# The k/q stage, the sum of z and the attention loop of a transformer block's backward pass, rearranged

## The chip, the cores and the metric

The kernel runs on one core of one Trainium2 chip. The metric is the time of one execution on the device in microseconds (us), the median of several runs. A core has five engines with their own instruction queues: TensorE (matmuls; PE in the profile, PEld its weight loads), VectorE (DVE), ScalarE (ACT), GpSimd (POOL) and SyncE (SP, which here issues transfers only). Sixteen DMA engines move data between DRAM and SBUF, the on-chip memory; matmul results go to PSUM.

## The reference, cut to what matters

The reference computes a pre-norm block and all its gradients: linear attention, then a SwiGLU feed-forward part (FFN), each on a layernorm without weights, with residuals. S = 2048 rows, D = 640, 32 heads of 20, F = 1728, all bf16.

```python
def _A_ref(x, wqkv, wo):
    ...                                        # q, k, v of 32 heads
    phi = lambda t: jnp.where(t > 0, t + 1, jnp.exp(t)) + 1e-6
    pq, pk = phi(q), phi(k)
    kv  = jnp.einsum("bhsd,bhse->bhde", pk, v)
    z   = jnp.einsum("bhsd->bhd", pk)          # sum of pk over the 2048 rows
    num = jnp.einsum("bhqd,bhde->bhqe", pq, kv)
    den = jnp.einsum("bhqd,bhd->bhq", pq, z)[..., None] + 1e-6
    return (num / den) ... @ wo

h   = x + _A_ref(_layernorm(x), wqkv, wo)
out = h + (silu(_layernorm(h) @ w_gate) * (_layernorm(h) @ w_up)) @ w_down
# results: out, and by jax.vjp with grad_out the gradients of x, wqkv, wo, w_gate, w_up, w_down
```

## The kernel before, where the change touches it

The rows are 16 tiles of 128. The kernel never forms v or the attention output: with xn the normalised x, Y = xn^T pk (`ps_y`), the masked blocks of Wv^T Y give kv (`ps_kvt`), those times wo give one matrix W2 (`ps_w2t`), and attention is then the normalised q times W2 (`ps_a`). A "dm step" (`ps_dm`) is a matmul of the backward pass, grad_out times w_down transposed, that depends on nothing here and is strewn in: 24 steps of 10 matmuls in all. PSUM has four tiles named `mm`, given out in turn, so a matmul group can start only when the group four places earlier has been read out.

The k/q stage, tile by tile. Tiles up to 10 have their normalised x transposed by TensorE (`copy1`), the last five by a DMA transpose that SyncE issues. The dictionary `after` sets at which tile SyncE issues the stores and the later loads.

```python
XD = 11
BY_V = (1, 2, 3, 6, 9)
...
def kq_mm(t, which, between=None, pieces=((0, DT),)):
    ...                                  # 10 matmuls ps_kq of 320 columns
    nc.scalar.activation(out=half(dst[:, t, :]), in_=row(ps), func=ACT.Exp, scale=sc)
    nc.scalar.activation(out=half(rr[...]), in_=row(ps), func=ACT.Relu, scale=sc)

def phi(which, t, n=2):
    e = (pk, pqa)[which][:, t:t + n, :]
    nc.vector.tensor_scalar(out=e, in0=e, scalar1=1.0, scalar2=1e-6, op0=ALU.min, op1=ALU.add)
    nc.vector.tensor_tensor(out=e, in0=e, in1=rr[...], op=ALU.add)
...
def copy1(t):                            # ln1_tr1: 5 transposes ps_t by TensorE
    (nc.vector.tensor_copy if t in BY_V else nc.scalar.copy)(out=xnT[:, t], in_=ln1_tr1(t))
...
for t in range(2, ST):
    ...
    if XD <= t + 2 < ST:
        ln1_xn(t + 2)
        nc.sync.dma_start_transpose(out=xnT[:, t + 2], in_=xn[:, t + 2, :])
    if t > 3 and t + 3 < ST:
        ln1_stats(t + 3)
    kq_mm(t, 0, (lambda: copy1(t + 1)) if t + 1 < XD else None)
    ...
    kq_mm(t, 1)
    ...                                  # phi of the tiles before; last: phi(0, 15), phi(1, 12), phi(1, 14)
    if t + 2 < XD:
        ln1_xn(t + 2)
    ...
    for f, *a in after.get(t, ()):
        f(*a)
```

Y and z. z is summed by TensorE, in four groups of 32 columns side by side; a second small matmul spreads it to all partitions (`zb`). `normalise` divides four tiles of q by their denominators, all on VectorE; `tr_pqs` transposes them by DMA.

```python
def normalise(t):
    ...                                  # tz = pq * zb (bf16), 4 tiles = 2560 elements
    nc.vector.tensor_reduce(out=den[:], in_=hb4(tz), axis=AX.X, op=ALU.add)
    nc.vector.tensor_scalar(out=den[:], ..., scalar1=1e-6, op0=ALU.add)
    nc.vector.reciprocal(out=rall[:, t:t + 4, :], in_=den[:])
    nc.vector.tensor_tensor(out=hb4(pq), in0=hb4(pq), in1=bc4(rall[:, t:t + 4, :]), op=ALU.mult)
...
def z_sum():
    ...                                  # 32 matmuls, lhsT=ones[:, :H], rhs=pk[:, t, n0:n1]
    nc.scalar.copy(out=half(zs[0][:]), in_=row(ps))
    nc.vector.tensor_tensor(out=half(zs[1][:]), in0=row(ps), in1=half(zs[0][:]), op=ALU.subtract)
    nc.vector.memset(KVT, 0.0)

for i in range(DT):                      # 5 column tiles of Y
    ...                                  # 32 matmuls ps_y; z_sum() after the first 16 of i = 0
    if i == 0:
        ...                              # ps_zb: 4 matmuls with ones32 (1/32), then zb
        masks()
    if 0 < i < 4:
        dm(1)
dm(1)
for t in (0, 4):
    normalise(t); tr_pqs(t)
for t in range(6):
    load_xr(t)
...                                      # kv_blocks: 4 x ps_kvt, each masked by VectorE into KVT
dm(1)
for i in range(DT):
    if i % 2 == 0 and i > 0:
        dm(1)
    ...                                  # ps_w2t, read out by ScalarE, transposed by DMA into W2
for t in (8, 12):
    normalise(t); tr_pqs(t)
dm(2)
```

The attention loop, which also makes the second layernorm (`hn`) and its transpose (`hnT`), the FFN's input:

```python
hnT = big.tile(...)
for t in range(ST + 2):
    if t < ST:
        ...                              # 10 matmuls ps_a; at t = 0 dm(1) between its halves
        nc.vector.tensor_tensor(out=half(xr[:]), in0=row(ps), in1=half(xr[:]), op=ALU.add)
        ln_stats(xr[:], mv[:, 0, :]); ln_rstd(mv, rstd2, t, 1)
        if t > 0:
            dm(1)
    if t > 2:
        load_xr(t + 3)
    u = t - 2
    ...
    nc.scalar.dma_start(out=scr_h1_v[:, u, :], in_=h1[:])
    nc.vector.tensor_scalar(out=hn[:, u, :], ...)
    nc.sync.dma_start_transpose(out=hnT[:, :, u * P:(u + 1) * P], in_=hn[:, u, :])
...
wgu = {0: load_wgu(0)}                   # the FFN's first weights
```

Of the kernel before, what the change touches and what calls it, by code (L numbers as in the profile page):

```python
# [20 lines left out]
def kernel(  # L21
# [160 lines left out]
    def load_wgu(g):  # L182
        w = GW[g]
        t = wpool.tile([P, DT, 2 * GM], BF16, name="wgu", tag="wgu")
        nc.sync.dma_start(out=t[:, :, 0:w], in_=B_w_gate[:, GO[g]:GO[g] + w].rearrange("(k p) n -> p k n", p=P))
        nc.sync.dma_start(out=t[:, :, w:2 * w], in_=B_w_up[:, GO[g]:GO[g] + w].rearrange("(k p) n -> p k n", p=P))
        return t
# [30 lines left out]
    def load_3():  # L218
        for t0 in range(4, ST, 2):
            yield load_x(nc.sync, t0, t0 + 2)  # L220
        yield load_wdT(wdT, 0)
        yield load_dh2T(0)
        yield load_dh2T(1)

    def load_dh2T(c):
        return nc.sync.dma_start_transpose(out=dh2T[:, :, c * 512:(c + 1) * 512], in_=go_flat[c * 512:(c + 1) * 512, :])

    def load_wv():
        nc.sync.dma_start(out=wvo[:, 0:5], in_=A_wqkv[:, 2 * D:3 * D].rearrange("(k p) n -> p k n", p=P))

    def load_wo(j0, j1):
        for j in range(j0, j1):
            nc.sync.dma_start(out=wvo[:, 5 + j, :], in_=A_wo[OH[j]:OH[j] + P, :])
# [9 lines left out]
    ones32 = const.tile([P, P], BF16, name="ones32")  # L243
    nc.vector.memset(ones32[:], 1.0 / H)
# [23 lines left out]
    XD = 11  # L268
    BY_V = (1, 2, 3, 6, 9)
# [46 lines left out]
    def phi(which, t, n=2):  # L316
        e = (pk, pqa)[which][:, t:t + n, :]
        nc.vector.tensor_scalar(out=e, in0=e, scalar1=1.0, scalar2=1e-6, op0=ALU.min, op1=ALU.add)
        nc.vector.tensor_tensor(out=e, in0=e, in1=rr[:, 2 * which + t // 2 % 2, t % 2:t % 2 + n, :], op=ALU.add)

    def store_k(c):
        nc.sync.dma_start(out=scr_pk_v[:, 4 * c:4 * c + 4, :], in_=pk[:, 4 * c:4 * c + 4, :])

    def store_q(c):
        nc.sync.dma_start(out=scr_pq_v[:, 4 * c:4 * c + 4, :], in_=pqa[:, 4 * c:4 * c + 4, :])

    def store_x(c):
        nc.sync.dma_start(out=scr_xnT[4 * c:4 * c + 4].rearrange("t p k c -> p t k c"), in_=xnT[:, 4 * c:4 * c + 4])

    after = {5: [(store_q, 0), (store_x, 0)], 6: [(load_dh2T, 2)], 7: [(load_dh2T, 3)], 8: [(load_wv,)], 9: [(store_q, 1)],  # L330
             10: [(store_x, 1)], 11: [(load_wo, 0, 2)], 12: [(load_wo, 2, 4)], 13: [(load_wo, 4, 6), (store_q, 2), (store_x, 2)],
             14: [(store_x, 3), (store_k, 0), (store_k, 1)],
             15: [(store_k, 2), (load_wdT, wdT, 1), (store_q, 3), (store_k, 3), (load_wdT, wdT3, 3)]}

    PIECES = ((0, 3), (3, DT))

    with tc.manual_schedule(engines={EngineType.PE, EngineType.DVE, EngineType.Activation, EngineType.Pool, EngineType.SP}):

        ps = mm("ps_warm")

        def warm(n):
            for _ in range(n):
                nc.tensor.matmul(ps[:, 0, :P], lhsT=ident[:], rhs=ident[:], start=True, stop=True)

        def copies(t, eng_copy):
            for sl, src in ln1_tr(t):
                c = eng_copy(out=xnT[:, t, sl], in_=src)
                if t == 0 and sl.start == 0:
                    wait_for(c, load_3())

        def copy1(t):
            (nc.vector.tensor_copy if t in BY_V else nc.scalar.copy)(out=xnT[:, t], in_=ln1_tr1(t))

        warm(37)
        ln1_stats(0)
        ln1_centre(0, 0, 3 * P)
        ln1_centre(0, 3 * P, D)
        copies(0, nc.scalar.copy)
        warm(8)
        ln1_stats(1)  # L360
        ln1_centre(1)
        kq_mm(0, 0, lambda: copies(1, nc.vector.tensor_copy), PIECES)
        ln1_stats(2)
        ln1_centre(2)
        kq_mm(1, 0, None, PIECES)
        ln1_stats(3)
        kq_mm(0, 1, lambda: copy1(2), PIECES)
        phi(0, 0)
        ln1_xn(3)
        kq_mm(1, 1)  # L370
        for t in range(2, ST):
            if t == 2:
                ln1_stats(4)
            if XD <= t + 2 < ST:
                ln1_xn(t + 2)
                nc.sync.dma_start_transpose(out=xnT[:, t + 2], in_=xn[:, t + 2, :])
            if t > 3 and t + 3 < ST:
                ln1_stats(t + 3)
            kq_mm(t, 0, (lambda: copy1(t + 1)) if t + 1 < XD else None)
            if t == 2:  # L380
                ln1_stats(5)
            if t == 3:
                ln1_stats(6)
            if t == ST - 1:
                phi(0, t - 1, 1)
            kq_mm(t, 1)
            if t == 3:
                phi(1, 0)
            elif t == ST - 1:
                phi(0, t, 1)  # L390
                phi(1, t - 3)
                phi(1, t - 1)
            elif t > 3:
                phi(t % 2, t - 2 - t % 2)
            if t + 2 < XD:
                ln1_xn(t + 2)
            if ST - NC - 1 <= t < ST - 1:
                ln1_xn(t - ST + NC + 1)
            for f, *a in after.get(t, ()):
                f(*a)  # L400

    fA.close()
    fpool = wB.enter_context(tc.tile_pool(name="fpool", bufs=6))
# [33 lines left out]
    def masks():  # L439
        tc.keep_in_program_order(nc.gpsimd.memset(mask[:], 1.0))  # L440
        for c0, n, p0 in ((0, 6, 0), (120, 2, 88)):
            m = mask[:, c0:c0 + n * Dh]
            for sign in (1, -1):
                tc.keep_in_program_order(nc.gpsimd.affine_select(
                    out=m, in_=m, pattern=[[-sign * Dh, n], [0, Dh]], compare_op=ALU.is_ge, fill=0.0,
                    base=-p0 if sign > 0 else p0 + Dh - 1, channel_multiplier=sign))
# [10 lines left out]
    def normalise(t):  # L457
# [7 lines left out]
        nc.vector.reciprocal(out=rall[:, t:t + 4, :], in_=den[:])  # L465
        nc.vector.tensor_tensor(out=hb4(pq), in0=hb4(pq), in1=bc4(rall[:, t:t + 4, :]), op=ALU.mult)

    def tr_pqs(t):
        for tt in range(t, t + 4):
# [9 lines left out]
    with tc.manual_schedule(engines={EngineType.PE, EngineType.DVE, EngineType.SP}):  # L479
        yk = strips.tile([P, DT * D + HG * P], BF16, name="yk", tag="S")  # L480
        Yt = yk[:, :DT * D].rearrange("p (k n) -> p k n", k=DT)
        KVT = yk[:, DT * D:].rearrange("p (j c) -> p j c", j=HG)
        zs = [wk("zs"), wk("zl")]

        def z_sum():
            ps = mm("ps_z")
            for ci, (n0, n1) in enumerate(NCH):
                for t in range(ST):
                    q = t % 4 * H
                    nc.tensor.matmul(ps[q:q + H, ci, :320], lhsT=ones[:, :H], rhs=pk[:, t, n0:n1],  # L490
                                     start=(t < 4), stop=(t >= ST - 4))
            nc.scalar.copy(out=half(zs[0][:]), in_=row(ps))
            nc.vector.tensor_tensor(out=half(zs[1][:]), in0=row(ps), in1=half(zs[0][:]), op=ALU.subtract)
            nc.vector.memset(KVT, 0.0)

        for i in range(DT):
            ps = mm("ps_y")
            for ci, (n0, n1) in enumerate(NCH):
# [3 lines left out]
                if (i, ci) == (0, 0):  # L502
                    z_sum()
            nc.scalar.copy(out=half(Yt[:, i, :]), in_=row(ps))
            if i == 0:
                ps_z = mm("ps_zb")
                mm_row(ps_z, lambda k: ones32[:], lambda k, n0, n1: zs[k][:, n0:n1], 2)
                nc.scalar.copy(out=half(zb[:]), in_=row(ps_z))
                masks()
# [3 lines left out]
        for t in (0, 4):  # L513
            normalise(t)
            tr_pqs(t)
# [14 lines left out]

        kv_blocks(KVT, "ps_kvt", lambda i, a, b: wv[:, i, a:b], lambda i, a, b: Yt[:, i, a:b])

# [3 lines left out]
        for i in range(DT):  # L536
# [5 lines left out]
            nc.sync.dma_start_transpose(out=W2[:, :, i * P:(i + 1) * P], in_=W2T[:, i, :])  # L542
        for t in (8, 12):
            normalise(t)
            tr_pqs(t)
        dm(2)

        hn = big.tile([P, ST, D], BF16, name="hn", tag="B")
        hnT = big.tile([P, DT, S], BF16, name="hnT", tag="B")
        h1s = {}  # L550
        for t in range(ST + 2):
            if t < ST:
# [11 lines left out]
                ln_rstd(mv, rstd2, t, 1)  # L564
                h1s[t] = (xr, mv)
                if t > 0:
                    dm(1)
            if t > 2:
                load_xr(t + 3)
            u = t - 2  # L570
# [9 lines left out]
            nc.scalar.dma_start(out=scr_h1_v[:, u, :], in_=h1[:])  # L580
            nc.vector.tensor_scalar(out=hn[:, u, :], in0=h1[:], scalar1=mv[:, 0, 0:1],
                                    scalar2=rstd2[:, u:u + 1], op0=ALU.subtract, op1=ALU.mult)
            nc.sync.dma_start_transpose(out=hnT[:, :, u * P:(u + 1) * P], in_=hn[:, u, :])


    with tc.manual_schedule(engines={EngineType.SP}):
# [7 lines left out]
        wgu = {0: load_wgu(0)}  # L594
# [7 lines left out]
        for g in range(4):  # L602
# [4 lines left out]
            for t in range(0, ST, 2):  # L607
# [25 lines left out]
                if g == 0 and t == 2:  # L633
                    wait_for(sig, load_dh2())
                    wgu[1] = load_wgu(1)
# [20 lines left out]
            elif g == 1:  # L656
                wgT[0] = big.tile([P, 14, D], BF16, name="wgT", tag="B")
                for gg in range(2):
                    tr_wgT(gg)
                    wgu[gg + 2] = load_wgu(gg + 2)  # L660
# [404 lines left out]
```

## Time and profile before

| | |
|---|---|
| time, median of 3 runs | 820.14 us (818.99 to 820.23) |
| span of the profiled execution | 818.3 us |
| mean granted clock of TensorE | 0.997 of full |
| instructions | 13931 |

The stages in the trace, by the first matmul of each (us from the start of the span):

| stage | from | to |
|---|---|---|
| loads and first k/q tiles | 0 | 11 |
| k/q stage, tiles 2 to 10 | 11 | 39.7 |
| k/q stage, tiles 11 to 15 | 42.0 | 57.4 |
| Y, z, four dm steps | 57.4 | 88.6 |
| kv blocks, W2, five dm steps | 88.6 | 101.0 |
| attention loop, 15 dm steps | 101.0 | 148.9 |
| FFN and all of the backward pass | 148.9 | 818.3 |

How to read what follows: a line of the chain of waits has a start, a length and an instruction group. A line of the list of waits says who waited for whom, then total us, times and the longest. In the table by stretches each engine has its busy us and, in brackets, its instructions. L308 is line 308 of the kernel. The end of a matmul is modelled, and matmuls overlap, so the time from start to start is what one costs TensorE's queue.

### The profile page before, as it was taken

The numbers are of one execution on the slowest core, as the hardware profiler recorded it, in microseconds if no ns is written. First come the engines' busy times: TensorE is split into PE (matmuls) and PEld (weight loads), VectorE is DVE, ScalarE is ACT, GpSimd is POOL, SyncE is SP. The second block draws the span as 40 slices with busy tenths as digits, with TensorE's granted clock in tenths as the row PEclk, the third lists the DMA queues.
The fourth block names the chain that finished last, engine by engine and source line by source line (L and its number), as shares of the span: only waits on it lengthen the run. The fifth ranks groups of instructions, "written<-read, shape, count | busy, mean of one in ns | idle before, by whom it ended". The sixth has DMA issues, their size and how long they took to land.

```text
span 818.3 us, 13931 instructions
## 1 busy us (share of the span) xinstructions
PE 811.3 (99%) x5515; PEld 521.0 (64%) x5515; DVE 442.2 (54%) x848; ACT 287.3 (35%) x402; POOL 193.3 (24%) x350
## 2 busy tenths in 40 slices
PE   9999999999999999999999999999999999999998
PEld 7666666555555555555566677777777777777675
DVE  7868687891077018810660147787793366631212
ACT  6962432670184126500741122322322133322010
POOL 3420022222412311221125501211220111112330
PEclk9999999999999999999999999999999999999999
DMA  9998779899659986995497747977498999999992
GB/s 256 220 311 180 161 165 298 208 264 210 178 127 216 220 200 136 205 251 113 100 230 199 262 110 218 224 201 186 104 246 173 173 146 192 169 192 241 204 226 77
DMA packets 281680, 159.43 MB, mean 195 GB/s; under 512 B 238412, under 2 KB 268237, under 8 KB 281616
## 3 DMA queue, kind: packets, MB, share of 16 engines
q1 hardware_dynamic: 255056, 82.94, 55.4%
q0 software_dynamic: 17744, 64.45, 25.2%
q10 hardware_dynamic: 8816, 11.16, 4.4%
q8 instruction: 43, 0.70, 0.4%
q14 instruction: 21, 0.17, 0.1%
HBM read 47.68 MB, written 53.66 MB: 124 GB/s over the span
## 4 chain that ended last, share of the span: by engine, by line
PE 97%; DMA 2%; DVE 1%; SPq 0%; issue 0%; DVEq 0%
PE ps_dw L683 21%; PE ps_dhn L109 14%; PE ps_dxn L935 8%; PE ps_o L997 7%; PE pg L611 7%; PE pu L616 7%; PE ps_dwqk L109 5%; PE ps_dm L414 5%; PE ps_kq L308 4%; PE ps_y L500 3%; PE ps_gt L742 3%; PE ps_a L557 3%; PE ps_dk L109 3%; PE ps_dp L109 3%; PE pdm L414 2%; DMA xnT<-xn 1%
## 5 line engine op out<-in xcount | busy, mean ns | idle before, releaser
L109 PE MATMUL ps_dhn<-wgT,cols 128*128 128x320 bf16 x864 | 119.5, 299 | 0.0
L683 PE MATMUL ps_dw<-dd,hn 128*128 128x448 bf16 (+1 forms) x640 | 118.8, 346 | 0.0
L109 PEld LDWEIGHTS <-cols 128*128 128x128 bf16 x864 | 84.5, 98 | 32.9
L683 PEld LDWEIGHTS <-hn 128*128 128x128 bf16 x640 | 62.6, 98 | 54.2
L685 DVE CAST dwev<-ps_dw 128x896 bf16<-128x896 f32 (+3 forms) x12 | 10.9, 908 | 123.6 <-PE ps_dw L683 123.6
L685 ACT CAST dwev<-ps_dw 128x896 bf16<-128x896 f32 (+1 forms) x20 | 17.6, 879 | 157.6 <-PE ps_dw L683 157.6
L648 POOL DMA_DIRECT2D scr_dT<-stg x64 | 34.6, 541 | 160.2 <-DMA stg<-dd 160.0
L147 DVE CUSTOM_DVE_ANT_0 lb_a<-lb_dy,hn 128x640 bf16<-128x640 bf16 x32 | 26.4, 825 | 76.1 <-ACT lb_dy L145 76.1
L611 PE MATMUL pg<-wgu,hnT 128*128 128x448 bf16 (+1 forms) x320 | 63.6, 346 | 0.0
L616 PE MATMUL pu<-wgu,hnT 128*128 128x448 bf16 (+1 forms) x320 | 63.6, 346 | 0.0
L997 PE MATMUL ps_o<-wd,mT 128*128 128x320 bf16 (+3 forms) x462 | 61.1, 295 | 0.0
L683 PE MATMUL ps_dw<-m_s,dh 128*128 128x448 bf16 (+1 forms) x320 | 60.4, 346 | 0.0
L935 PEld LDWEIGHTS <-ring 128*128 128x128 bf16 x480 | 47.0, 98 | 18.2
L997 PEld LDWEIGHTS <-mT 128*128 128x128 bf16 (+1 forms) x462 | 41.8, 97 | 17.4 <-issue 2.6
L935 PE MATMUL ps_dxn<-wqkvT,ring 128*128 128x320 bf16 x320 | 51.3, 299 | 0.0
L308 PE MATMUL ps_kq<-wqk,xnT 128*128 128x320 bf16 x320 | 47.3, 306 | 2.5 <-DMA xnT<-xn 2.3
L616 PEld LDWEIGHTS <-hnT 128*128 128x128 bf16 x320 | 31.3, 98 | 27.1
L683 PEld LDWEIGHTS <-dh 128*128 128x128 bf16 x320 | 31.3, 98 | 27.1
L611 PEld LDWEIGHTS <-hnT 128*128 128x128 bf16 x320 | 31.3, 98 | 27.0
L414 PE MATMUL ps_dm<-wdT,dh2T 128*128 128x448 bf16 (+1 forms) x240 | 47.0, 344 | 0.0
L414 PEld LDWEIGHTS <-dh2T 128*128 128x128 bf16 x320 | 31.0, 98 | 24.8
L145 ACT ACTIVATE lb_dy<-ps_dhn,rstd 128x640 bf16<-128x640 f32 x16 | 12.7, 794 | 88.6 <-PE ps_dhn L109 88.6
(167 smaller groups left out, 1269.3 us busy)
## 6 DMA issues: line engine op xcount, KB each, us to landing
scr_dT<-stg POOLq DMA_DIRECT2D x48, 224.0 KB, 3.7
cols<-scr_dT POOLq DMA_DIRECT2D x6, 1728.0 KB, 8.9
scr_m<-m_s POOLq DMA_DIRECT2D x12, 448.0 KB, 4.7
cols<-scr_dT ACTq DMA_DIRECT2D x2, 1728.0 KB, 8.5
out_dram<-dwev POOLq DMA_DIRECT2D x30, 112.0 KB, 3.2
scr_dT<-stg POOLq DMA_DIRECT2D x16, 192.0 KB, 2.8
scr_pq<-pqa SPq DMA_DIRECT2D x4, 640.0 KB, 4.9
scr_xnT<-xnT SPq DMA_DIRECT2D x4, 640.0 KB, 5.6
```

The lines of the kernel that those rows point to most:

```text
L109: nc.tensor.matmul(ps[:, ci, :320], lhsT=lhs(k), rhs=rhs(k, *NCH[ci]), start=(start and k == 0), stop=(stop and k == n - 1))
L147: nc.vector.tensor_tensor_reduce(out=a[:], in0=dy[:], in1=xhat, scale=1.0, scalar=0.0, op0=ALU.mult, op1=ALU.add, accum_out=sums[:, 1:2])
L308: nc.tensor.matmul(ps[:, ci, :320], lhsT=xnT[:, t, k, :], rhs=wqk[:, k, w0 + n0:w0 + n1], start=(k == 0), stop=(k == DT - 1))
L414: nc.tensor.matmul(ps[:, c, :w], lhsT=dh2T[:, kt, (t + c) * P:(t + c + 1) * P], rhs=wdT[:, kt, o:o + w], start=(kt == 0), stop=(kt == DT - 1))
L500: nc.tensor.matmul(ps[:, ci, :320], lhsT=xn[:, t, i * P:(i + 1) * P], rhs=pk[:, t, n0:n1], start=(t == 0), stop=(t == ST - 1))
L611: nc.tensor.matmul(pg[:, c, :w], lhsT=hnT[:, kt, (t + c) * P:(t + c + 1) * P], rhs=wg[:, kt, 0:w], start=(kt == 0), stop=(kt == DT - 1))
L616: nc.tensor.matmul(pu[:, c, :w], lhsT=hnT[:, kt, (t + c) * P:(t + c + 1) * P], rhs=wg[:, kt, w:2 * w], start=(kt == 0), stop=(kt == DT - 1))
L648: nc.gpsimd.dma_start(out=scr_dT[t + c, :, KO[g]:KO[g] + GK[g], :], in_=stg[:, :GK[g], :])
L683: nc.tensor.matmul(ps[:, c, :w], lhsT=lhs(t), rhs=rhs(t), start=(t == 0), stop=(t == ST - 1))
L685: last = copy(out=ev[:, :len(parts), :w], in_=ps[:, :len(parts), :w])
L935: nc.tensor.matmul(ps[:, ci, :320], lhsT=lhs[:, i, :], rhs=rhs[:, i, n0:n1], start=(k == 0 and i == 0), stop=(k == 2 and i == DT - 1))
L997: nc.tensor.matmul(po(t, ci), lhsT=mTs[t // 4][r, t % 4, j, :], rhs=wd[r, j, n0:n1], start=(t, ci) not in opened, stop=last)
```

## The change

In the k/q stage it gives up the DMA transposes of the last five tiles: all tiles go over TensorE, PSUM and a copy by ScalarE (VectorE for tile 12 too). SyncE's order there is left to the scheduler, with all loads queued after the first tile. z is summed by VectorE in fp32 from pk, two tiles at a time, in place of 32 matmuls, and TensorE spreads it to the partitions after the third column tile of Y instead of the first. `normalise` is split into denominators and product, so that work for the kv blocks can come between. Three dm steps move from the attention loop to ahead of it (twelve there instead of nine). In the loop the FFN's weights are loaded in two pieces, the last four q tiles are transposed one per iteration, h1 is stored from GpSimd, and the hn transposes follow by hand-set lags. It is meant to keep transposes and transfers off each other's way and to take the sum of z off TensorE.

```diff
-    XD = 11
-    BY_V = (1, 2, 3, 6, 9)
+    BY_V = (1, 2, 3, 6, 9, 12)
...
     def load_3():
         for t0 in range(4, ST, 2):
             yield load_x(nc.sync, t0, t0 + 2)
+        yield nc.sync.dma_start(out=wvo[:, 0:5], in_=A_wqkv[...])
+        for j in range(HG):
+            yield nc.sync.dma_start(out=wvo[:, 5 + j, :], in_=A_wo[...])
         yield load_wdT(wdT, 0)
-        yield load_dh2T(0)
-        yield load_dh2T(1)
+        for c in range(4):
+            yield nc.sync.dma_start_transpose(out=dh2T[...], in_=go_flat[...])
+        yield load_wdT(wdT, 1)
+        yield load_wdT(wdT3, 3)
...                                       # phi stores pk, q and xnT itself, after each fourth tile; "after" goes
         for t in range(2, ST):
-            if XD <= t + 2 < ST:
-                ln1_xn(t + 2)
-                nc.sync.dma_start_transpose(out=xnT[:, t + 2], in_=xn[:, t + 2, :])
-            kq_mm(t, 0, (lambda: copy1(t + 1)) if t + 1 < XD else None)
+            kq_mm(t, 0, (lambda: copy1(t + 1)) if t + 1 < ST else None)
...
             elif t == ST - 1:
-                phi(0, t, 1)
-                phi(1, t - 3)
-                phi(1, t - 1)
+                last_phi = phi(0, t, 1)
...
+        z2 = tzs[:, 4:8].rearrange("p t d -> p (t d)").bitcast(FP32)
+        zf = z2[:, :D]
+        tok2 = pk.rearrange("p (t two) d -> p t (two d)", two=2)
+        with tc.issue_after(last_phi):
+            nc.vector.tensor_tensor(out=z2, in0=tok2[:, 0], in1=tok2[:, 1], op=ALU.add)
+        for t in range(2, ST // 2):
+            nc.vector.tensor_tensor(out=z2, in0=z2, in1=tok2[:, t], op=ALU.add)
+        nc.vector.tensor_tensor(out=zf, in0=zf, in1=z2[:, D:], op=ALU.add)
+        nc.vector.tensor_copy(out=zs[0][:], in_=zf)
+        nc.vector.tensor_tensor(out=zs[1][:], in0=zf, in1=zs[0][:], op=ALU.subtract)
+        for t in (ST - 4, ST - 2):
+            phi(1, t)
+        nc.vector.memset(KVT, 0.0)
+        masks()
...
-                if (i, ci) == (0, 0):
-                    z_sum()
+                if (i, ci) == (2, 1):
+                    z_bcast()             # 4 matmuls ps_zb with ones, then zb by ScalarE
...
-        for t in (0, 4):
-            normalise(t)
-            tr_pqs(t)
+        norm_den(0)
+        norm_mul(0)
+        tr_pqs(0)
+        norm_den(4)
...                                       # kv_blocks
+        norm_mul(4)
...                                       # W2
+        tr_pqs(4)
         for t in (8, 12):
-            normalise(t)
-            tr_pqs(t)
-        dm(2)
+            norm_den(t)
+            norm_mul(t)
+            if t < 12:
+                tr_pqs(t)
+        dm(5)
...                                       # attention loop
-                if t > 0:
+                h1_todo.append((t, xr))
+                if t > 0 and t % 4 != 3:
                     dm(1)
+            if t in (7, 9):
+                load_wgu(0, t // 9)
+            while h1_todo and h1_todo[0][0] < t:
+                v, h1 = h1_todo.pop(0)
+                nc.gpsimd.dma_start(out=scr_h1_v[:, v, :], in_=h1[:])
             if t > 2:
                 load_xr(t + 3)
+            if t < 4:
+                tr_pqs(12 + t, 1)
+            if t == 3:
+                hnT = big.tile([P, DT, S], BF16, name="hnT", tag="B")
...
-            nc.scalar.dma_start(out=scr_h1_v[:, u, :], in_=h1[:])
-            nc.sync.dma_start_transpose(out=hnT[:, :, u * P:(u + 1) * P], in_=hn[:, u, :])
+            hnT_todo.append(u)
+            for v in hnT_todo[:0 if t < 4 else 1 if t < 14 else 3]:
+                hnT_todo.pop(0)
+                nc.sync.dma_start_transpose(out=hnT[:, :, v * P:(v + 1) * P], in_=hn[:, v, :])
```

## The prediction

> **What bounds the kernel now.** I read the page first: engine table, chain, costliest groups. Then the list of waits for TensorE alone, then the first 150 us: the stretches around the one wait, the chain in order of time, and the timelines of VectorE, ScalarE and SyncE.
>
> The page gives the frame. TensorE is busy for 811.3 of 818.3 us and the chain that ended last is 97% TensorE:
>
> ```profile
> PE 811.3 (99%) x5515; PEld 521.0 (64%) x5515; DVE 442.2 (54%) x848; ACT 287.3 (35%) x402; POOL 193.3 (24%) x350
> ...
> PE 97%; DMA 2%; DVE 1%; SPq 0%; issue 0%; DVEq 0%
> ```
>
> So a change is worth what it takes off TensorE's queue or adds to it, plus the waits of TensorE that it removes or makes. The waits are soon listed; these are all of the whole program:
>
> ```profile
> PE ps_kq L308 <- DMA xnT<-xn: 2.3, 1, 2.3
> PE ps_warm L343 <- POOL ident masks.py:199: 1.4, 1, 1.4
> ```
>
> The first lies exactly in the part that the change takes out: tile 11 is the first of the five whose transposed x comes by DMA. The stretches around it show that it costs more than its own length (columns: stretch, its length, busy us and count of each engine, granted clock, DMA share, GB/s):
>
> ```profile
> 40.00:42.00 2.00, 0.00 (x0) 0.00 (x0) 1.54 (x3) 1.16 (x2) 1.19 (x1) 1.00 1.17 320
> 42.00:44.00 2.00, 1.99 (x9) 1.19 (x10) 1.86 (x5) 0.00 (x0) 1.08 (x2) 0.61 1.12 362
> 44.00:46.00 2.00, 2.00 (x9) 1.16 (x8) 1.51 (x6) 1.30 (x2) 0.45 (x1) 0.54 1.15 338
> 46.00:48.00 2.00, 2.00 (x17) 1.46 (x15) 1.79 (x4) 1.33 (x3) 1.78 (x4) 1.00 1.26 216
> ```
>
> After the gap TensorE runs about four microseconds at 0.54 to 0.61 of its clock: 9 matmuls in 2 us instead of 17 or so. The chain gives the pieces for the sum (start, length, what):
>
> ```profile
> 26.38 0.28 PE ps_t L299 x5
> 26.66 2.72 PE ps_kq L308 x20
> ...
> 42.01 15.43 PE ps_kq L308 x100
> 57.44 2.17 PE ps_y L500 x16
> 59.62 1.20 PE ps_z L490 x32
> 60.82 2.28 PE ps_y L500 x16
> 63.10 0.54 PE ps_zb L109 x4
> ```
>
> The reader should take from it: one k/q tile is 2.72 us (0.136 us a matmul), five transposes on TensorE are 0.28 us, the sum of z is 1.20 us, and after 42.01 there is no gap to the end.
>
> **What the Trainium skill says.** "TensorE: Matmul & The Clock Gate", section "What's actually happening": the clock gate halves the array's clock after an idle window and gives it back after a busy one of about 3.4 us. The trace agrees with the halved clock and the length of the recovery (42 to 46 us), though here a gap of only 2.3 us was enough. "VectorE: DVE Perf Modes", section "The perf-mode tier table": a two-tensor operation on bf16 runs at 2x and on fp32 at 1x, a copy of fp32 at 2x. The trace agrees for what it has: 2560 elements of bf16 multiplied take 1486 ns, the same number at 1x (with an fp32 operand) 2826 ns. "TensorEngine Tiling (Array Packing)", section "Available Configurations": stationary operands of 32 columns let four tiles work side by side. The trace agrees: the 32 matmuls of z take 1.20 us, 37 ns each, against 136 ns for a full one of the same 320 columns. So the old sum of z was already cheap, and removing it brings little.
>
> **The change part by part.**
>
> (1) The x of tiles 11 to 15 is transposed by TensorE again. Added to TensorE: 5 x 0.28 = +1.4 us. Removed: from the end of tile 10's matmuls (39.72) to the start of y (57.44) the trace has 17.72 us for 100 matmuls that need 100 x 0.136 = 13.6; the loss is 4.1 us, 2.3 of it the wait and 1.8 the low clock. That holds only if ScalarE and VectorE keep pace with the added copies. ScalarE: four activations at 0.585 us start to start plus a copy at 0.59 are 2.93 us a tile, TensorE needs 2.72 + 0.28 = 3.00. That is what tiles 4 to 8 show now (copies at 26.70 and 29.69, no wait of TensorE). VectorE: statistics 1.04, xn 0.36, two phi operations 1.28, in all 2.7 us; xn of tile 11 would be ready near 37.5, TensorE wants it near 38.2. So I count −4.1 + 1.4 = −2.7, and y starts at about 54.7. Call that point Y.
>
> (2) The 32 matmuls of z leave TensorE: −1.2 us. The broadcast (0.54) stays, two tiles of y later.
>
> (3) VectorE now adds pk up. Seven additions of 1280 elements with an fp32 result: by the table at 1x; from the 2826 ns for 2560 elements at 1x (about 160 ns of it fixed) one is 1.49 us, and since each needs the one before, 1.52 start to start: 10.6. The last fold of 640 is 0.85, the copy to bf16 about 0.5, the subtraction 0.85: 12.9 us together. It starts when the last phi of pk is done, by the pattern of 56.86 to 57.94 and with ScalarE a little behind, Y + 0.9; so zl is there at Y + 13.8. TensorE comes to the broadcast after three tiles of y and one dm step: 3 x 4.35 + 1.89 = Y + 14.9. Hidden, with 1.1 us to spare.
>
> (4) What follows it is less free. VectorE then does two late phi pairs (2.7) and the memset (0.4), to Y + 17.0, while zb is there at Y + 14.9 + 0.5 + 0.8 = Y + 16.2. Denominators of tiles 0 to 3, their product and denominators of 4 to 7: one full normalise is 64.45 to 72.82 = 8.4, a denominator alone 8.4 − 2.8 = 5.6: together 14.0, to Y + 31.0. TensorE ends y at 5 x 4.35 + 0.54 + 4 x 1.89 = Y + 29.9; its kv blocks end at Y + 31.3 and the next dm step wants the first block's PSUM tile back, which VectorE can mask only at Y + 31.3. I put 0.3 us of waiting there. Then the masks are done at about Y + 32.6 and the W2 matmuls come at Y + 33.4: no wait.
>
> (5) Five dm steps instead of two directly ahead of the loop, three fewer in it (the old loop's last call did nothing): the 24 steps stay 24, no TensorE time. They give the W2 transposes 9.5 us of cover (5 x 1.89) where 3.8 was already enough.
>
> (6) Loop: the last normalise ends on VectorE near Y + 52; the first result of ps_a waits for it from Y + 49 and blocks TensorE only at the third iteration, Y + 54.7. Today's 107.10 against 107.5 is just as close and costs nothing. In the iterations without dm TensorE needs 1.36 us, VectorE 2.2 to 2.3, but over four iterations it is 4 x 1.36 + 3 x 1.63 = 10.3 against 9.2, and four PSUM tiles carry the difference. The FFN weights were already issued at 126.32 and 128.67, in the loop, so issuing them in two pieces is a rearrangement; the same for the hn transposes, of which the late ones are needed only when the FFN comes to its last pair, 7 x 3.79 us after its start. Storing h1 from GpSimd instead of ScalarE frees an engine that isn't the bound ("DMA: Bandwidth & Descriptors", section "Issuing engines are not separate DMA queues": they share the same 16 engines; no run here isolates it).
>
> Sum: −4.1 + 1.4 − 1.2 + 0.3 = −3.6 us. From 820.1 to **816.5 us**, −0.4%.
>
> **The rivals.** A: the sum on VectorE is late and becomes the new wait in place of the DMA's. For it: only 1.1 us of slack at the broadcast and none at the kv blocks, and the price of a mixed bf16/fp32 addition is an estimate. Against it: all of VectorE's shapes at 1x in this trace agree within 2% with the same formula. If the chain is 3 us longer TensorE waits about 3.3 us in all, and the time is about 819.5; if the gap also halves the clock for 4 us, about 821.
>
> B: ScalarE becomes the bound of the k/q stage. For it: 2.93 of 3.00 us a tile, and three tiles in a row with copies. Each 0.1 us a tile over 3.0 costs half a microsecond: 817.
>
> C: SyncE's queue. All weights, dh2 and the down projection are now queued at the start, ahead of the stores of q and x; 16 transposes of the normalised q follow later. For it: DMA engines are full in this stage (share 1.00 to 1.04), and one transpose takes 1.2 to 1.7 us of the queue. Against it: the first dm step comes at Y + 8.7 and the weights for v and wo at Y + 30, and the transposes now have more cover. If pqsT is late the loop waits a few us: 819 to 822.
>
> D: the 2.3 us wait was only hiding another, so that removing it gives nothing back: 820. The timelines of ScalarE and VectorE speak against it: ScalarE idles 3.35 us for TensorE there.
>
> **The range and the chances.** The certain terms (−1.2 and +1.4) nearly cancel, so the sign hangs on the 4.1 us and on whether A or C eats it. Eight times in ten between 814.8 and 820.0. Two per cent is 16.4 us; everything that the change touches on TensorE's path is below 6 us, so within 2%: 0.97; faster 0.01, slower 0.02 (a chain of late transposes with low clock behind each).
>
> **What would show it right or wrong.** Right: no wait of TensorE on xnT; ps_t with 25 more transposes (80 in all); clock 1.00 from 30 us on; y starting near 54.7; ps_z gone; seven additions of about 1.49 us; the FFN's first matmul near 145.3 instead of 148.94. Wrong on (3) and (4): a wait of TensorE at ps_zb on VectorE, or at ps_dm or ps_w2t after the kv blocks, longer than half a microsecond. Wrong on C: a wait of ps_a, ps_dm or pg on a DMA. After the FFN's start all stages should keep their lengths; a difference there would be something that I haven't seen.

## The result, and the profile after

| | before | after |
|---|---|---|
| time, median of 6 runs each | 819.77 us (818.77 to 820.23) | 815.91 us (815.75 to 816.21) |
| ratio, 95% interval | | 0.9955 (0.9942 to 0.9968) |
| span of the profiled execution | 818.3 us | 814.3 us |

The change makes the kernel 0.45% faster: 3.9 us where 3.6 were predicted, and inside the range. The page of the changed kernel, its engine table and its chain:

```profile
PE 809.8 (99%) x5508; PEld 520.7 (64%) x5508; DVE 453.2 (56%) x857; ACT 288.1 (35%) x405; POOL 200.4 (25%) x366
...
PE 99%; POOL 0%; ACT 0%; issue 0%; DVE 0%; POOLq 0%
```

The 2% of the chain that were DMA are gone (5.1 us of them were a load of weights at the start, 5.5 us the transpose of tile 11). TensorE's busy time is 1.5 us less, where the slow matmuls after the old gap count in full. TensorE's list of waits has only the start-up wait left:

```profile
PE ps_warm L333 <- POOL ident masks.py:199: 1.6, 1, 1.6
```

The chain in order of time (start, length, what) gives the stage borders:

```profile
50.91 4.08 PE ps_kq L304 x30
54.98 8.69 PE ps_y L491 x64
...
69.91 0.54 PE ps_zb L109 x4
...
84.83 1.43 PE ps_kvt L512 x30
86.26 1.90 PE ps_dm L394 x10
...
145.18 1.89 PE pg L617 x10
```

Set against the chain of before, whose y starts at 57.44, kv blocks at 88.59 and FFN at 148.94:

| stretch | before | after | difference |
|---|---|---|---|
| start of the span to start of y | 57.44 | 54.98 | −2.46 |
| y to the kv blocks | 31.15 | 29.85 | −1.30 |
| kv blocks to the FFN | 60.35 | 60.35 | 0.00 |
| FFN to the end | 669.36 | 669.12 | −0.24 |

Sum −4.0, the difference of the spans. The last row is scatter, and so is part of the first: TensorE's transposes of tile 10, the last ones ahead of what the change touches, start at 35.21 us before and at 35.48 after (35.1 to 35.8 in the traces of all runs). From there to y it is 22.07 us before and 19.34 after, −2.7. VectorE's timeline shows why nothing new is waited for (start, length, line, operation, count):

```profile
55.67 1.48 DVE L470 TENSOR_TENSOR tzs<-pk 128x1280 f32<-128x1280 bf16 x1
57.19 9.12 DVE L472 TENSOR_TENSOR tzs<-tzs,pk 128x1280 f32<-128x1280 f32 x6
...
67.73 0.83 DVE L476 TENSOR_TENSOR zl<-tzs,zs 128x640 bf16<-128x640 f32 x1
...
84.42 0.95 DVE L445 RECIPROCAL rall<-den 128x128 f32<-128x128 f32 x1
85.29 1.40 DVE L515 TENSOR_TENSOR yk<-ps_kvt,mask 128x120 bf16<-128x120 f32 x4
```

zl is finished at 68.56 and TensorE asks for it at 69.91: 1.35 us of slack. The first of the four masks (`yk`) is done at 85.5, and the dm step that takes over its PSUM tile starts at 86.1 in TensorE's timeline: about 0.6 us.

### The profile page after: what moved, and what is told of

Its sections match the earlier page's. It is cut to its first block, busy times and chain, and to the rows that moved or that the text cites. A ratio compares the mean times of both kernels' runs of the same rounds, so it can differ in the third digit from the quotient of the medians.

```text
span 814.3 us, 13916 instructions
## 1 busy us (share of the span) xinstructions
PE 809.8 (99%) x5508; PEld 520.7 (64%) x5508; DVE 453.2 (56%) x857; ACT 288.1 (35%) x405; POOL 200.4 (25%) x366
## 4 chain that ended last, share of the span: by engine, by line
PE 99%; POOL 0%; ACT 0%; issue 0%; DVE 0%; POOLq 0%
PE ps_dw L689 22%; PE ps_dhn L109 14%; PE ps_dxn L941 8%; PE ps_o L1003 7%; PE pu L622 7%; PE pg L617 7%; PE ps_kq L304 5%; PE ps_dwqk L109 5%; PE ps_dm L394 5%; PE ps_dk L109 3%; PE ps_gt L748 3%; PE ps_y L491 3%; PE ps_dp L109 3%; PE ps_a L549 3%; PE pdm L394 2%; PE ps_warm L333 1%
```

## The experiments

Four kernels at a time shared one chip with the kernel before. A ratio is always to the kernel before on that chip; microseconds against the changed kernel are differences of medians.

### The k/q stage alone

The kernel before, all tiles transposed by TensorE:

```diff
-    XD = 11
-    BY_V = (1, 2, 3, 6, 9)
+    XD = ST
+    BY_V = (1, 2, 3, 6, 9, 12)
```

> The kernel before with one thing changed: all 16 tiles of x are transposed by TensorE (tile 12's copy on VectorE), everything else as before. My theory: most of the gain is here. The wait of 2.3 us and the low clock after it go (-4.1 us), 25 transposes of 0.056 us come (+1.4 us): 2.7 us faster than before, about 817.1 us; y starts near 55 us in the trace. Rival (the removed wait only hid another, or ScalarE becomes the bound of the stage): no gain, 820 us, with TensorE waiting on a copy by ScalarE.

Measured 817.77 us against 819.95, ratio 0.9978 (0.9960 to 0.9997). Its timeline of TensorE starts y at

```profile
54.83 2.34 PE L500 MATMUL ps_y<-pk,xn 128*128 128x320 bf16 x16
```

where the same view of before has 57.28: 2.45 us earlier. Step (1) carries most of the gain. The rival (nothing is won, or ScalarE takes over) falls: the stretches from 40 to 46 us run at clock 1.00 without a wait, and no other wait comes in the place of the one removed.

### What made the transpose late

The kernel before with only the order of SyncE's queue changed:

```diff
     def load_3():
         ...
+        yield load_wv()
+        yield from load_wo(0, HG)
         yield load_wdT(wdT, 0)
-        yield load_dh2T(0)
-        yield load_dh2T(1)
+        for c in range(4):
+            yield load_dh2T(c)
...
-    after = {5: [(store_q, 0), (store_x, 0)], 6: [(load_dh2T, 2)], ...
+    after = {13: [(store_q, 0), (store_x, 0), (store_q, 1), (store_x, 1), (store_q, 2), (store_x, 2)],
+             14: [(store_x, 3), (store_k, 0), (store_k, 1)],
+             15: [(store_k, 2), (load_wdT, wdT, 1), (store_q, 3), (store_k, 3), (load_wdT, wdT3, 3)]}
```

> The kernel before, the last five tiles still transposed by DMA, but SyncE issues the weights for v and o and all of dh2 straight after x, and the stores of q, x and k only after tile 13, so that nothing else is issued among the five transposes. If the wait comes from the transpose being queued behind other transfers, it goes: 4.1 us faster than before, about 815.7 us, with no transposes added to TensorE. If it comes from xn being normalised too late for a DMA transpose (two tiles ahead), the wait stays at about 2 us and the time at 818 to 820 us.

Measured 822.03 us, ratio 1.0026 (1.0016 to 1.0037): slower. Yet the mechanism is the first of the two. The transpose of tile 11 is issued at 35.15 and has landed 2.8 us later; before it was issued at 36.48 and took 5.5 us, with a load of weights issued just ahead of it and still under way. So it lands 4.0 us earlier, 1.3 of it by its turn in the queue and the rest by the time to landing. There is no wait on xnT, y starts at 53.44, and the waits of TensorE, besides start-up, are

```profile
PE ps_a L558 <- DMA wvo<-wvo: 2.7, 1, 2.7
```

The reason is in SyncE's timeline:

```profile
62.98 8.25 SPq L260 DMA_TRANSPOSE wdT<-in_B_w_down_dram  x1
...
77.28 11.25 SPq L471 DMA_TRANSPOSE pqsT<-pqa  x8
88.58 4.05 SPq L478 DMA_DIRECT2D xr<-in_A_x_dram  x6
...
93.25 7.69 SPq L543 DMA_TRANSPOSE wvo<-wvo  x5
```

The postponed stores and loads push the first q transposes to 77.28 (72.97 before). SyncE reaches W2's transposes at 93.25, no earlier than before (93.49), although TensorE is 3.8 us ahead of its old times there; it is ready for the loop at 97.1 and waits until 99.8, and then the three stretches from 100 to 106 us have 0.79, 0.50 and 0.86 of the clock. The late xnT was a matter of the order in the queue, and the queue took the time back one stage later.

### z on VectorE alone, and with the rest of the change

The first kernel is the one before with VectorE's sum, the later broadcast and the split `normalise`, nothing of the loop:

```diff
+        with tc.issue_after(last_phi):
+            nc.vector.tensor_tensor(out=z2, in0=tok2[:, 0], in1=tok2[:, 1], op=ALU.add)
+        ...
-                if (i, ci) == (0, 0):
-                    z_sum()
+                if (i, ci) == (2, 1):
+                    z_bcast()
...
-            normalise(t)
+            norm_den(t)
+            norm_mul(t)
```

> The kernel before with z summed by VectorE and broadcast after the third column tile, normalise split as in the change; the DMA transposes of the last five tiles and the loop stay as before. My theory: only the 1.2 us of the 32 matmuls go, about 818.6 us, with the wait on xnT and the low clock still there and no wait at ps_zb or after the kv blocks. Rival (VectorE is too late): a wait of TensorE at ps_zb or ps_dm of 0.5 to 3 us, 819 to 822 us.

Measured 823.47 us, ratio 1.0040 (1.0024 to 1.0056). Slower than either theory allowed, and not where the rival looked: there is no wait at ps_zb or after the kv blocks. TensorE's waits:

```profile
PE ps_kq L308 <- DMA xnT<-xn: 2.3, 1, 2.3
PE ps_dm L410 <- ACT dmst L424: 2.2, 2, 2.0
PE ps_warm L343 <- POOL ident masks.py:199: 1.4, 1, 1.4
PE ps_dm L410 <- ACT dm L424: 1.0, 1, 1.0
PE ps_a L564 <- DMA wvo<-wvo: 0.5, 1, 0.5
```

The new ones, 3.7 us, are all in the attention loop. SyncE has 12 q transposes in one row there, 16.1 us from 100.01 on, and what it issues behind them comes late: the first load of x in the loop at 121.70 instead of 117.81, for which VectorE idles 4.1 us. But TensorE does not wait for VectorE. It waits for ScalarE's read-outs of dm steps, and ScalarE has the stores of h1 in order ahead of them. Two of these stores stand for long (SyncE's lines are from its own timeline):

```profile
115.36 5.71 ACTq L587 DMA_DIRECT2D scr_h<-xr  x2
135.58 0.33 ACTq L587 DMA_DIRECT2D scr_h<-xr  x1
```

```profile
116.15 0.58 SPq L583 DMA_DIRECT2D scr_KVT<-yk  x1
130.34 0.39 SPq L185 DMA_DIRECT2D wgu<-in_B_w_gate_dram  x1
```

The second store of the first line is issued at 120.75, though VectorE had its row ready at 117.5; the last one at 135.58, though its row was ready at 132.0. In the trace each waits for a semaphore that tells of the landing of another transfer: the store of KVT that SyncE issued at 116.15, right behind the q transposes (landed 120.69), and the load of the FFN's first weights issued at 130.34 (landed 135.51). The read-outs follow at 121.12 and 135.95, and TensorE's dm steps, 1.0 and 2.0 us late, behind them. In the kernel before the stores of h1 wait for landings in the same way (120.70 behind a load of x landed at 120.61), but early enough to cost TensorE nothing.

The second kernel is the complement: all of the change except the k/q stage.

```diff
-    BY_V = (1, 2, 3, 6, 9, 12)
+    XD = 11
+    BY_V = (1, 2, 3, 6, 9)
...                                  # DMA transposes of tiles 11 to 15, and "after" with its loads and stores, as before
```

> The changed kernel with the k/q stage of before: the last five tiles by DMA transpose, loads and stores strewn in as before; the sum of z by VectorE, the split normalise, dm steps and loop of the change stay. If the two halves of the change add up, it is 1.2 us faster than before (the 32 matmuls), 818.6 us, with the wait on xnT there. Rival: the second half needs the first (a later y makes SyncE late for W2 and x): waits in the loop, 820 us or more, as with z on VectorE alone.

Measured 819.14 us against 819.85, ratio 0.9995 (0.9987 to 1.0002). The point is 0.7 us below before, not clear of noise, and below the 1.2 us expected. Part of the shortfall is the low clock after the gap: 17 of its 21 runs show it by a mean clock of 0.998 or less, against 19 of the 41 of before beside it. Among runs at 0.999 or more it is 1.1 us below before (817.85 against 818.95), among the others 0.75 (819.31 against 820.06). The trace has no wait in the loop; besides start-up only

```profile
PE ps_kq L311 <- DMA xnT<-xn: 2.3, 1, 2.3
```

The pair shows what the rearrangement of the loop, with the dm steps and q transposes moved along with it, is for: with it VectorE's sum costs nothing, without it the kernel is 3.5 us slower.

### The split of normalise

The changed kernel with `norm_mul(4)` moved back in front of the kv blocks:

```diff
         norm_den(4)
+        norm_mul(4)
...
-        norm_mul(4)
```

> The changed kernel with the split undone: the product for tiles 4 to 7 is done before the kv blocks' masks again, 2.8 us more of VectorE's work in front of them. My theory: VectorE masks the first kv block at about 88.0 instead of 85.3 us, and TensorE's next dm step, which wants that PSUM tile at 86.3, waits 2.0 us: 818 us if the clock holds, up to 820 us if this gap halves the clock for 4 us as the gap of 2.3 us did before. Rival (that order does not matter, a PSUM tile or other slack covers it): 816 us, as the changed kernel.

Measured 819.25 us, ratio 0.9989 (0.9978 to 1.0000): 3.3 us worse than the changed kernel. TensorE's waits, then its timeline:

```profile
PE ps_dm L394 <- DVE yk L516: 2.2, 1, 2.2
```

```profile
88.77 2.75 PE L394 MATMUL ps_dm<-wdT,dh2T 128*128 128x448 bf16 x10 [2.22 <-DVE yk L516]
91.32 1.27 PE L128 MATMUL ps_w2t<-yk,wvo 128*128 128x120 bf16 x14
```

The wait is 2.2 us as reckoned, and behind it ten matmuls take 2.75 us where 2.06 are usual. The 14 runs fall into two groups, seven at 817.8 to 818.4 with mean clock 1.000 and seven at 820.1 to 820.9 with 0.998: the gap costs about 2 us always and about 2.3 more when the clock falls (medians 818.1 and 820.3).

### How much slack the sum has

The changed kernel with three more additions, into memory that nothing reads before it is overwritten:

```diff
+        zx = tzs[:, 0:4].rearrange("p t d -> p (t d)").bitcast(FP32)
+        for t in range(3):
+            nc.vector.tensor_tensor(out=zx, in0=z2, in1=tok2[:, t], op=ALU.add)
```

> The changed kernel with three more additions of 1280 fp32 elements in VectorE's sum, into memory that nothing reads; 4.4 us more in front of zl. It measures the slack of step (3). By the trace zl is ready at 68.6 us and TensorE asks for it at 69.9, so TensorE should wait 3.0 us at ps_zb, and up to 1.8 us more where the gap halves the clock: 819 us, or 820.7 with the low clock, in two groups of runs as the whole-normalise run had. Rival A's mirror (the sum is hidden deeper than I think, so it costs nothing): 816 us.

Measured 820.57 us, ratio 1.0013 (1.0006 to 1.0019), 4.6 us above the changed kernel beside it. Seven runs with clock 1.000 lie at 820.0 to 820.2, the other fourteen at 820.5 to 823.3. TensorE's waits:

```profile
PE ps_zb L109 <- DVE zs L478: 2.4, 1, 2.4
...
PE ps_dm L394 <- DVE yk L518: 0.6, 1, 0.6
PE ps_zb L109 <- DVE zl L479: 0.5, 1, 0.5
```

2.9 us at the broadcast as reckoned, and 0.6 after the kv blocks, which was not. Three additions take 4.55 us, so the first figure puts the slack at 1.6 us. Rival A's danger was real; the original sum just fits.

### The parts of the loop

The changed kernel with h1 stored from ScalarE again:

```diff
-                nc.gpsimd.dma_start(out=scr_h1_v[:, v, :], in_=h1[:])
+                nc.scalar.dma_start(out=scr_h1_v[:, v, :], in_=h1[:])
```

> The changed kernel with h1 stored from ScalarE's queue again. My step (6): it frees an engine that isn't the bound, so 816 us as the changed kernel. Rival, from the run with z on VectorE alone (waits of 1.0 and 2.0 us of TensorE's dm steps on ScalarE's read-out in the loop): the stores sit in ScalarE's queue ahead of the read-outs of PSUM and hold them up: waits of ps_dm on ScalarE, 817 to 820 us.

Measured 817.23 us (815.91 to 818.46), ratio 0.9959 (0.9944 to 0.9974): by the intervals not told apart from the changed kernel, though six of its seven runs (816.54 and more) lie above all six of the changed one, on another chip. The profiled run, its longest, has the rival's wait:

```profile
PE ps_dm L394 <- ACT dmst L408: 1.3, 2, 0.7
```

The longer of the two, 0.7 us, comes about as in the run with z on VectorE alone: the store of h1 ahead of the read-out is issued at 131.31, when the FFN's first weights, issued by SyncE at 124.89, have landed (131.23), though its row was ready at 127.5.

The changed kernel with the q transposes all ahead of the loop and each hn transpose issued at once (hnT is allocated ahead of the loop):

```diff
-            if t < 12:
-                tr_pqs(t)
+            tr_pqs(t)
...
-            for v in hnT_todo[:0 if t < 4 else 1 if t < 14 else 3]:
+            for v in hnT_todo[:1]:
```

> The changed kernel with all q transposes issued ahead of the loop and each hn transpose issued in the iteration of its hn, as before the change. My step (6): a rearrangement, 816 us. Rival: SyncE then waits for hn in every iteration, the loads of x behind it come late, VectorE waits for x and TensorE for a PSUM tile: waits of ps_dm or ps_a in the loop, 817 to 820 us.

Measured 818.18 us, ratio 0.9974 (0.9965 to 0.9984), whose interval just meets the changed kernel's (0.9942 to 0.9968): 2.3 us more by the medians, on different chips. The profiled run, with 816.84 us one of its shortest, waits for VectorE, and the chain there runs through a load of x that landed after 6.05 us:

```profile
PE ps_dm L394 <- DVE xr L553: 0.7, 1, 0.7
```

The changed kernel with two dm steps ahead of the loop instead of five:

```diff
-        dm(5)
+        dm(2)
...
-                if t > 0 and t % 4 != 3:
+                if t > 0:
```

> The changed kernel with two dm steps instead of five ahead of the loop (and one in every iteration). My step (5) took the order of the dm steps as free: 816 us. Rival, from the run with z on VectorE alone (0.5 us of waiting on the transposes of W2): the later denominators leave W2 and VectorE too late for a loop that starts 5.7 us earlier; TensorE waits 0.5 to 1.5 us on W2's transpose at ps_a and perhaps again in the loop: 817 to 819 us.

Measured 816.25 us, ratio 0.9955 (0.9939 to 0.9972): the same as the changed kernel. No wait on W2; 0.3 us on VectorE in the loop, and 0.8 us on a load in the FFN, in the profiled run, which at 818.0 was the longest.

### Both gains together

The changed kernel with the last five tiles on DMA transposes again, in the queue order of the run in which the wait vanished:

```diff
-    BY_V = (1, 2, 3, 6, 9, 12)
+    XD = 11
+    BY_V = (1, 2, 3, 6, 9)
...
+    after = {13: [(store_q, 0), (store_x, 0), (store_q, 1), (store_x, 1), (store_q, 2), (store_x, 2)],
+             14: [(store_x, 3), (store_k, 0), (store_k, 1)],
+             15: [(store_k, 2), (load_wdT, wdT, 1), (store_k, 3), (load_wdT, wdT3, 3)]}
```

> The changed kernel, but the last five tiles' x goes by DMA transposes again, with nothing else issued among them (the order of loads and stores of the run in which the wait on xnT vanished). My theory: 25 transposes leave TensorE (-1.4 us) and no wait comes back, since the z chain and the five dm steps leave SyncE until about 80 us for its stores: 814.5 us, faster than both kernels. Rival: SyncE's queue is then late for W2 or for the q transposes, as it was in that run (2.7 us of waiting and a low clock): 817 to 820 us.

Measured 815.18 us against 820.01, ratio 0.9941 (0.9925 to 0.9957). It was then run beside the changed kernel itself (both unaltered, so without a diff).

> The changed kernel, unaltered, on the same chip as the three that follow, as their common measure: 815.9 us, 0.9955 of the kernel before, by both theories.

Measured 815.95 us, ratio 0.9956 (0.9942 to 0.9969).

> The kernel of e8 again, beside the changed kernel. If taking the 25 transposes off TensorE is worth its 1.4 us less the waits that e8's trace shows (0.2 us on xnT, 1.0 us at ps_a), it is 0.5 to 1.0 us faster than the changed kernel, about 815.1 us. Rival: e8's lower time was the chip, and the two are equal.

Measured 815.22 us, ratio 0.9946 (0.9933 to 0.9958). Besides start-up it waits for

```profile
PE ps_t L287 <- DVE xn L276: 0.3, 1, 0.3
PE ps_a L560 <- DVE xr L564: 0.2, 1, 0.2
```

Twice about 0.7 us below the changed kernel, and four of its five runs (814.91 to 815.34) are below all five of the changed one (815.64 to 816.78). The ratios' intervals overlap, so this is likely rather than shown. From the transposes of tile 10 to y the stage takes 18.34 us against the changed kernel's 19.34, so 1.0 of the 1.4 us is there. Some of it is lost again in the loop, where loads of x and the FFN's weights land late: kv blocks to FFN take 60.70 us here and 61.56 in the trace of the first time, against 60.35.

## Why the prediction was right

**What bounds the kernel.** Right: the difference of the spans is the sum of what left TensorE's queue and of the wait removed; the FFN and everything after it kept their length within 0.24 us.

**Step (1), −2.7.** Right in mechanism, and right in size for a run with the low clock. From tile 10's transposes to y the traces differ by 2.7 us; the run of that part alone is 2.2 us faster by the medians. The term that was mis-sized is the 1.8 us of low clock: it was read from one profiled execution as if every run had it. Of the 41 runs of the kernel before that went with the first four experiments, 20 have a mean clock of 0.999 or 1.000 and a median of 819.1 us, 21 have 0.998 or less and 820.25 us. So the low clock comes in about half of the runs and is worth 1.1 us there. In the trace of the kernel with the k/q stage of before and the rest of the change, which kept its clock, the same stretch takes 20.66 us: without the low clock step (1) is worth 1.3 us. The 2.3 us of waiting are in every trace that has the DMA transposes in the old order. ScalarE kept pace, as reckoned: its idle time before the copies was 0 to 0.34 us (rival B falls, and so does D, since no other wait appeared).

**Steps (2) and (3), −1.2 and hidden.** Right: 1.30 us in the trace, of which 1.20 is ps_z. The chain of VectorE was put at 12.9 us (its parts add up to 12.8) and took 55.67 to 68.56, 12.9; seven additions at 1.49 were measured at 1.48 and, each waiting for the one before, 1.52 from start to start. This agrees with the Trainium skill, "VectorE: DVE Perf Modes", section "The perf-mode tier table" (fp32 at 1x, and the copy at 2x: 0.49 us for 640). The predicted slack of 1.1 us was 1.35.

**Step (4), +0.3.** The wait did not come. The denominators were finished at Y + 30.4 instead of Y + 31.0, because the sum started 0.2 us earlier and the memset overlapped. That the place is tight is shown by the whole-normalise run, where 2.8 us more of VectorE's work made a wait of 2.2; both figures give 0.6 us of slack.

**Step (5), no time.** Right: 816.25 us with the dm steps moved back. What was moved there for cover was not needed.

**Step (6), no time.** The sum was right (kv blocks to FFN: 60.35 us in both), the reason given was wrong. "A rearrangement" it is only for the kernel before, which had z early. With z on VectorE the kernel with the old loop is 3.5 us slower than before (823.47 against 819.95), with the rearranged one it is not (819.14 against 819.85). ScalarE is not the bound, but its queue empties PSUM for TensorE, and a store of h1 in it can stand until a transfer of SyncE has landed; GpSimd's queue has no such read-outs. Rivals A and C were right about where the danger lay: C's late transposes and loads appear in the queue as soon as the loop's order is undone. Of the parts undone one at a time, the q and hn transposes together matter most (818.18); which of the two is not shown, and for the store of h1 the time alone decides nothing.

**A reading of PSUM that was wrong.** The description of the kernel and steps (4) and (6) count the four PSUM tiles in turn. The trace of the run with z on VectorE alone contradicts that: its third ps_a starts while VectorE has not yet read out the first.

```profile
106.59 1.52 PE L564 MATMUL ps_a<-wvo,pqsT 128*128 128x320 bf16 x10
```

```profile
108.48 0.82 DVE L568 TENSOR_TENSOR xr<-ps_a,xr 128x640 bf16<-128x640 f32 x1
```

This fits a tile being given out again as soon as it is empty, here that of a dm step, which ScalarE had read out by 103.8. The margin of step (6) was therefore wider than it was reckoned.

**The sum.** That −3.6 came within 0.3 us of the measured −3.9 is partly luck. The 0.3 us of step (4) did not come, and the low clock was counted in full: against the runs of before that kept their clock (819.1) the change is worth about 3.2 us, against the others (820.25) about 4.3, and the median of before lies between.

## What to carry to other kernels

Where one engine is busy 99% of the span, count what leaves its queue, then ask of each new producer how long before the demand it is ready: here 1.35 us decided between a gain of 1.2 us and a loss. A transfer that is late because of its neighbours in an issuing queue can be mended by reordering the queue, but the neighbours must still go somewhere; look at the next stage's first transfer before calling it free. Ask also what else stands in the queue of the engine that empties PSUM: in the traces of the old loop with z on VectorE and of h1 stored from ScalarE, a store there, held up by another queue's transfer, made TensorE wait although that engine had little to do. And one part of a change measured alone can be worse than nothing, as the sum on VectorE was, while it pays together with the part that makes room for it.

## What the runs showed of the hardware that was not expected

A gap in TensorE's work of a little over two microseconds lowers its clock in some executions and not in others, at the same place in the same program. The profiled execution of before had 0.61 and 0.54 of the clock after its gap of 2.29 us; the kernel with the k/q stage of before and the rest of the change had a gap of 2.31 us and then this (columns as in the stretches of the prediction):

```profile
42.00:44.00 2.00, 1.51 (x12) 1.09 (x13) 1.86 (x6) 0.00 (x0) 0.64 (x2) 1.00 1.11 364
44.00:46.00 2.00, 2.00 (x17) 1.46 (x15) 1.54 (x4) 1.88 (x3) 0.90 (x1) 1.00 1.10 375
```

Seventeen matmuls in 2 us at full clock, against nine. How often the clock fell differs from kernel to kernel: in 21 of 41 runs of the kernel before and in 17 of 21 of this one, both with a gap of 2.3 us in their traces; in 7 of 14 with one of 2.2 us (the whole normalise) and in 18 of 22 with one of 2.7 us (the reordered queue). The Trainium skill, "TensorE: Matmul & The Clock Gate", section "What's actually happening", says that the window over which activity is counted runs freely and is 3.4 us long; a gap shorter than the window that trips it sometimes fits the first, but the lower clock after 2.2 and 2.3 us is sooner than the whole idle window that the section names, and the measurement decides. One profile of a kernel with such a gap can therefore mislead by 1.1 to 2.3 us either way; the mean clock of the single runs tells it.
